# The tail of the attention stage put in the order in which its inputs arrive

## The chip, the cores and the metric

The kernel runs on one core of a Trainium2 chip. The metric is device time in microseconds (us), from three runs of the kernel. One more execution was taken with the profiler; all rows shown here come from that one.

## What is computed

The input is q, k, v for 4 batches, 8 heads, 576 positions and 64 values per head. Three stages follow each other, all in float32:

```
attn  softmax(scale * q k^T) v     heads 0-3: the last 32 positions; heads 4-7: every 4th of the last 128
x     2304 tokens x 512            (batch and position together, heads side by side)
moe   e = argmax(x @ w_gate);  gate = softmax(x @ w_gate)[e];  og = sigmoid(x @ w_output_gate)[e]
      y[token] = gate * og * (relu(x @ w1[e]) @ w2[e])          8 experts, 512 -> 1024 -> 512
moe2  out = softplus(y @ w_in) @ w_out                          512 -> 2048 -> 512
```

## The kernel before

**Attention.** The tokens are cut into 20 tiles (4 batches of five tiles, the fifth with 64 rows). A loop over `i` from 0 to 21 works on three tiles at once: scores and softmax of tile `i`, the transposed probabilities and the values of tile `i - 1` (`transpose_p`, `values`, `normalise`), and the transposed output of tile `i - 2` (`transpose_x`, `evict_x`). So the last tile, 19, is transposed in step 21, the last. In most steps two to four units of the next batch's q and k are transposed too (`transpose_qk`). The order of the instructions on TensorE (PE), ScalarE (ACT), VectorE (DVE) and the DMA queue of SyncE (SP) is the order in which the code is written; each of these engines works its list off in that order.

**PSUM.** Of the eight banks two belong to the scores (`ps_s`), one to the values (`ps_o`) and five to a ring (`ps_t`) that takes, one after the other, the transposed q and k (`pqk`), probabilities (`pp`) and outputs (`px`), the logits (`pl`, `plt`) and the ranks of the router (`prk`).

**Routing.** The tiles are routed in six groups; the last, group 5, is tiles 17 to 19. For a group, `logits` and `route` turn the transposed x into logits, the chosen expert, the token's place within it (`places`) and its weight (`pair`), in some 25 small DVE operations with one transpose (`plt`) and five small matmuls (`prk`) between them. They run as generators; `pump()` takes a few steps of them at fixed points of the loop. `scatter_idx` then writes the places and weights to DRAM (`idx_dram`) in one indirect DMA per tile from GpSimd (POOL). For group 5 that was put off to the end of the tail (`deferred`).

**The first expert.** After group 2 the expert with most tokens is taken as rank 0. Its first 424 token columns are put together on PE, without a trip through DRAM for the late tokens: `mm_gathered` (L968) adds rows of early tiles that were gathered from DRAM (`xg`, four tiles `t` of up to 128 rows), multiplied by a diagonal matrix of their weights (`diag`); `mm_late` (L1020) adds the rows of the late tiles 14 to 19, which are loaded (`load_late`, `xl`), scaled and split in a high and a low half (`split_late`: `h` on ACT, `l` on DVE) and multiplied by a selection matrix (`sel_late`, `sel`, on DVE). Tiles 14 and 19 have 64 rows each and share one operand. The four sums, one per 128 of the 512 values, stand in four accumulators `xacc` of one bank each: two in `ps_s`, one in `ps_o`, one in the ring.

**After that** `split_rank0` copies the accumulators out as `xh` (ACT) and `xl` (DVE), and the first expert's matmuls (`ph`, L900 to L902) begin. `order` sorts the experts by size on DVE, in small pieces during rank 0 (`tabi` is its result); from it SP reads which weights (`wr`) and which indices (`idx`) rank 1 needs. Weights come in pieces of 512 KB; `piece_hi` (ACT, `wh`) and `piece_lo` (DVE, `wl`) split them, and each `piece_lo` lets SP load one more.

What stands in step 20 and 21 and the tail is set by a table of events (`at(...)`), and the tail by a list `late` behind the loop (L1209 on), which is worked off while `pump()` moves group 5 along.

Of the kernel before, what the change touches and what calls it, by code (L numbers as in the profile page):

```python
# [14 lines left out]
I32 = mybir.dt.int32  # L15
# [27 lines left out]
def attn_moe_softplus_kernel(ctx: ExitStack, tc: tile.TileContext, q, k, v, w_gate, w_ogate, w1, w2, w_in, w_out, out, dbg=None):  # L43
# [257 lines left out]
    def transpose_qk(b, half, ti, y):  # L301

        ps = ps_t.tile([P, 512], F32, tag="tp", name=f"pqk{b}{half}{ti}{y}")

        def to(t, y):
            dst = qT[b % 2][64 * y : 64 * y + 64, half] if t == 0 else kT[b % 2][64 * y : 64 * y + 64, half, :, y]
            return dst[:, :, :S].rearrange("q x (p j) -> q x p j", j=9)

        if y < 2:
            r = raw[b, half, ti].rearrange("p y e -> p (y e)")
            for j in range(4):
                c = 2 * D * (5 * y + j)
# [166 lines left out]
    def transpose_x(b, w):  # L481
        d = tl[b, w]
        x2 = d["x"].rearrange("q a h d -> q (a h d)")
        ps = ps_t.tile([P, 512], F32, tag="tp", name=f"px{b}{w}")
        for c in range(4):
            nc.tensor.transpose(ps[:, P * c : P * c + P], x2[:, P * c : P * c + P], identf)
        d["xp"] = ps
# [59 lines left out]
    def route(g):  # L547
# [14 lines left out]
        d, eq, ex, sel, pm = t3("rd"), t3("req"), t3("rex"), t3("rsel"), t3("rpm")  # L562
        oh = t3("roh", BF16)
        cb = K["rt"].tile([P, NE], F32, tag="rcb", name=f"rcb{g}")
        posi = t2("rposi", I32)
        V.tensor_copy(lg[:, js], xT.pop(g)[:, :G4])
        yield 0
        R(mx, L, AX.X, ALU.max)
# [113 lines left out]

    def order():
        V = nc.vector
        pc = K["px"][0].tile([P, 512], F32, tag=K["px"][1], name="pcnt")[:, :NE]
        nc.tensor.matmul(pc, ones, cumb[:, len(GROUPS)], start=True, stop=True)

        def o3(nm):
            return K["rt"].tile([1, NE, NE], F32, tag=nm, name=nm, bufs=1)

        def o2(nm, n=NE):
            return K["rt"].tile([1, n], F32, tag=nm, name=nm, bufs=1)

        cnt, key, rank, g, r, lt, tmp, tab = o2("ocnt"), o2("okey"), o2("orank"), o3("og"), o3("or_"), o3("olt"), o3("otmp"), o2("otab", 40)
        ov = K["rt"].tile([1, NE, NT // OVW], F32, tag="oov", name="oov", bufs=1)
        thr = K["rt"].tile([1, NE, NT // OVW], F32, tag="thr", name="thr", bufs=1)
        for i in range(NE):
            nc.gpsimd.iota(thr[:, i], [[OVW, NT // OVW]], base=CAPS[i], channel_multiplier=0, allow_small_or_imprecise_dtypes=True)
        E0 = eidx[0:1]
        V.memset(tab, 0.0)  # L700
        V.scalar_tensor_tensor(key, pc[0:1], float(NE), rev[0:1], ALU.mult, ALU.add)
        V.scalar_tensor_tensor(key, first[0:1], float(2 * NE * NT), key, ALU.mult, ALU.add)
        V.tensor_copy(cnt, pc[0:1])
        yield
# [132 lines left out]
    def ntile(n):  # L837
        return (n + P - 1) // P
# [111 lines left out]
        nc.vector.tensor_scalar(d_[:rows], identf[:rows], idx[0].bitcast(F32)[:rows, t, 1:2], None, ALU.mult)  # L950

    def acc(c):
        pool, tag = ((ps_s, "s"), (ps_s, "s"), (ps_o, "o"), (ps_t, "tp"))[c]
        xacc[c] = pool.tile([P, 512], F32, tag=tag, name=f"xacc{c}")

    def acc0(c):
# [4 lines left out]
    def mm_gathered(cs):  # L961
        for c in cs:
            if c not in xacc:
                acc0(c)
        for t in range(ntile(CAPS[0])):
            rows = min(P, CAPS[0] - P * t)
            for c in cs:
                nc.tensor.matmul(  # L968
                    xacc[c][:, P * t : P * t + rows],
                    xg[0, t][:rows, P * c : P * c + P],  # L970
                    xacc["d", t][:rows, :rows],
                    start=False,
                    stop=False,
                    skip_group_check=True,
                )

    def rows_of(i):
        return P if i % NW < NW - 1 else S % P
# [230 lines left out]
    def w_lo(i, j):  # L1209
        lo_(0, j)  # L1210

    late = []
    for c in (2, 3):
        late += [(mm_late, 15, (c,), (0,)), (mm_gathered, NL, (c,))]
    late += [(mm_late, 15, (c,), (1,)) for c in (2, 3)] + [(mm_late, 15, (c,)) for c in (0, 1)] + [(mm_late, 16, (c,)) for c in range(NC)]
    late += [(fn, i) for fn in (sel_late, split_late) for i in range(17, n)] + [(w_lo, 17, j) for j in (0, 1)]
    late += [(mm_late, 17, (c,)) for c in range(NC)]

    late += [(mm_late, i, (c,)) for i, c in ((n - 2, 0), (n - 2, 1), (n - 1, 0), (n - 1, 1), (n - 2, 2), (n - 1, 2), (n - 2, 3), (n - 1, 3))]
    while late:  # L1220
        if bg:
            pump()
        fn, i, *a = late[0]
        g = next(g for g, (t0, t1) in enumerate(GROUPS) if t0 <= i < t1)
        if fn is mm_gathered or all(e[2] != g for e in bg):
            late.pop(0)
            fn(*a) if fn is mm_gathered else fn(i, *a)
    for fn in deferred:
        fn()
# [303 lines left out]
```

## Time and profile before

| | |
|---|---|
| median of the three runs | 806.53 us (804.1 to 810.0) |
| profiled execution | 803.44 us, of which the span from the first to the last instruction is 801.8 us |
| busy share of the span | PE 95%, DVE 68%, ACT 60%, POOL 15% |
| TensorE clock, mean of the span | 0.98 of full speed |

A row of the timeline gives the start, the length, the engine, the source line, the operation and its tiles; in brackets, how long the engine stood idle before it and what ended that. "x8" says that eight instructions in a row are shown as one; a matmul of float32 operands shows as two. "PEclk" is the granted clock: 1.00 is 2.4 GHz, 0.50 is 1.2 GHz.

### The profile page before, as it was taken

The page shows a single profiled execution, that of the slowest core. Times are in us where ns is not written, and L with a number is a line of the kernel's source. Part 1 is how long each engine was busy: PE and PEld are TensorE (multiplying, and loading weights), DVE is VectorE, ACT ScalarE, POOL GpSimd, SP SyncE. Part 2 cuts the span into 40 slices and gives each one's busy share as a digit, 9 for nine tenths or more (in the row PEclk, how much of TensorE's full clock was granted, in tenths as well). Part 3 has the DMA queues.
Part 4 walks back from the last instruction along what each step waited for, and adds up shares of the span by engine and source line. Part 5 has one row for each costly group of instructions (what it writes and reads, how often), then busy time and mean ns, then how long its engine had stood idle before and what let it go on. Part 6 is the DMA issues. An engine that isn't in the chain of part 4 may idle for free.

```text
span 801.8 us, 15124 instructions
## 1 busy us (share of the span) xinstructions
PE 764.0 (95%) x5542; PEld 690.7 (86%) x5543; DVE 548.5 (68%) x1098; ACT 479.3 (60%) x935; POOL 119.9 (15%) x154
## 2 busy tenths in 40 slices
PE   6998886999999999999999999999999999999994
PEld 4666665898999999999989999999998999999993
DVE  6967885763667977885698877766656656656561
ACT  4776642344556666666798878655556555655551
POOL 9814343121002011100000000110000001001001
PEclk8999997799999999999999999999999999999997
DMA  9996766255789999879524211310000001001001
GB/s 236 266 248 171 147 161 150 79 184 188 239 273 292 315 304 320 294 249 306 173 80 132 78 47 41 119 40 20 1 14 27 0 1 40 1 1 40 1 1 39
DMA packets 87008, 106.60 MB, mean 133 GB/s; under 512 B 30524, under 2 KB 61500, under 8 KB 86912
## 3 DMA queue, kind: packets, MB, share of 16 engines
q1 hardware_dynamic: 75616, 86.32, 36.9%
q0 software_dynamic: 5104, 13.40, 5.2%
q10 hardware_dynamic: 6192, 5.56, 2.0%
q8 instruction: 65, 1.06, 0.6%
q14 instruction: 31, 0.25, 0.1%
HBM read 85.03 MB, written 20.37 MB: 131 GB/s over the span
## 4 chain that ended last, share of the span: by engine, by line
PE 69%; issue 8%; DVE 5%; ACT 3%; DMA 2%; POOL 0%; ACTq 0%; SPq 0%; POOLq 0%; DVEq 0%
PE pg L900 7%; PE pg L901 7%; PE pg L902 7%; PE q L1442 7%; PE q L1441 7%; PE q L1443 7%; PE py L896 3%; PE py L897 3%; PE py L898 3%; PE ph L896 3%; PE ph L898 2%; PE ph L897 2%; PE ph L900 1%; PE ph L902 1%; PE ph L901 1%
## 5 line engine op out<-in xcount | busy, mean ns | idle before, releaser
L900 PE MATMUL pg<-xhm,wh 128*128 128x384 f32 x384 | 129.5, 337 | 0.5 <-ACT l L1408 0.4
L901 PE MATMUL pg<-xlm,wh 128*128 128x384 f32 x384 | 129.6, 338 | 0.0
L902 PE MATMUL pg<-xhm,wl 128*128 128x384 f32 x384 | 129.4, 337 | 0.0
L733 DVE TENSOR_TENSOR wl<-wr,wh 128x1024 fp32r<-128x1024 f32 (+1 forms) x86 | 98.2, 1144 | 30.7 <-ACT wh L788 30.6
L1406 ACT ACTIVATE u<-pg 128x384 f32<-128x384 f32 x96 | 47.2, 492 | 116.5 <-PE pg L902 116.4
L1442 PE MATMUL q<-wl,gh 128*128 128x512 f32 x288 | 113.2, 393 | 0.0
L1441 PE MATMUL q<-wh,gh 128*128 128x512 f32 x288 | 113.0, 393 | 0.0
L1443 PE MATMUL q<-wh,gl 128*128 128x512 f32 x288 | 112.6, 391 | 0.0
L788 ACT CAST wh<-wr 128x1024 fp32r<-128x1024 f32 x74 | 77.2, 1047 | 15.1 <-ACT y L923 5.2
L1450 POOL DMA_INDIRECT out_dram<-o,perm_sb x18 | 18.1, 1004 | 435.9 <-DVE o L260 303.2
L1412 DVE TENSOR_SCALAR w<-u 128x384 f32<-128x384 f32 x68 | 24.6, 362 | 84.7 <-ACT u L1407 84.2
L900 PEld LDWEIGHTS pg<-xhm,wh 128*128 128x128 f32 x384 | 72.1, 188 | 5.0 <-ACT l L1408 1.1
L901 PEld LDWEIGHTS pg<-xlm,wh 128*128 128x128 f32 x384 | 72.0, 188 | 3.7
L902 PEld LDWEIGHTS pg<-xhm,wl 128*128 128x128 f32 x384 | 72.1, 188 | 0.0
L1414 DVE SCALAR_TENSOR_TENSOR u<-w,u 128x384 f32<-128x384 f32 x96 | 53.7, 560 | 21.6 <-ACT w L1410 19.3
L1443 PEld LDWEIGHTS q<-wh,gl 128*128 128x128 f32 x288 | 54.1, 188 | 12.3
L1441 PEld LDWEIGHTS q<-wh,gh 128*128 128x128 f32 x288 | 54.1, 188 | 8.6
L1442 PEld LDWEIGHTS q<-wl,gh 128*128 128x128 f32 x288 | 54.0, 188 | 8.2
L896 PE MATMUL ph<-xh,wh 128*128 128x392 f32 (+5 forms) x192 | 58.6, 305 | 1.6 <-ACT y L923 0.9
L1416 DVE TENSOR_TENSOR l<-l,u 128x384 f32<-128x384 f32 x96 | 53.5, 557 | 7.7 <-ACT w L1420 0.5
L896 PE MATMUL py<-hh,wh 128*128 128x312 f32 (+8 forms) x192 | 58.4, 304 | 0.0
L897 PE MATMUL py<-hl,wh 128*128 128x312 f32 (+4 forms) x192 | 57.3, 299 | 0.1
(205 smaller groups left out, 1746.3 us busy)
## 6 DMA issues: line engine op xcount, KB each, us to landing
wr<-in_moe_w_dram SPq DMA_DIRECT2D x64, 512.0 KB, 6.1
praw<-in_moe_w_out_dram SPq DMA_DIRECT2D x12, 512.0 KB, 5.8
raw<-in_q_dram SPq DMA_DIRECT2D x8, 576.0 KB, 6.9
raw<-in_k_dram SPq DMA_DIRECT2D x8, 576.0 KB
x2r<-yT_dram SPq DMA_DIRECT2D x12, 384.0 KB, 4.2
vP<-in_v_dram SPq DMA_DIRECT2D x16, 272.0 KB, 9.0
praw<-in_moe_w_in_dram SPq DMA_DIRECT2D x8, 512.0 KB
wr<-in_moe_w_in_dram SPq DMA_DIRECT2D x8, 512.0 KB, 3.3
```

Source lines behind the costliest of these rows:

```text
L733: e.tensor_tensor(lo, src, hi.bitcast(F32), ALU.subtract)
L788: (eng or nc.scalar.copy)(d[1], d[0])
L896: nc.tensor.matmul(ps if wide else ps[:, :cut], wh, xh if wide else xh[:, :cut], start=wide, stop=False, skip_group_check=True)
L897: nc.tensor.matmul(ps[:, :cut], wh, xl[:, :cut], start=False, stop=False, skip_group_check=True)
L900: nc.tensor.matmul(ps, wh, xh, start=(first and i == 0), stop=False)
L901: nc.tensor.matmul(ps, wh, xl, start=False, stop=False)
L902: nc.tensor.matmul(ps, wl, xh, start=False, stop=(last and i == k - 1))
L1414: nc.vector.scalar_tensor_tensor(u, w_, 1.0, u, ALU.subtract, ALU.subtract)
L1416: nc.vector.tensor_tensor(l, l, u, ALU.subtract)
L1441: nc.tensor.matmul(acc[b, t], gh[:, ts_], wh, start=(f == 0), stop=False)
L1442: nc.tensor.matmul(acc[b, t], gh[:, ts_], wl, start=False, stop=False)
L1443: nc.tensor.matmul(acc[b, t], gl[:, ts_], wh, start=False, stop=(f == NF - 1))
```

## The change

**Events instead of a list.** The list `late` behind the loop is gone. All its work stands as events of step 21, in a new order, and `mm_gathered` does one gathered tile `t` per call for the accumulators that it is given. The scaling of tiles 14 to 16 (`sp`) is moved from step 20 behind the transposed x of tile 19. Group 5 is moved along by counted steps (`go`) between the matmuls.

**Banks.** The ring `ps_t` has four banks. The eighth bank is a pool of its own, `ps_x0`, for every transposed x (`px`), for two units of q and k at the start, and for the fourth accumulator.

**Counts and indices.** The first part of `order`, with its matmul `pcnt`, stands ahead of tile 19's matmuls and takes its bank from the ring. `scatter_idx` of group 5 follows the places at once, with an index tile of its own.

```
-    ps_t = psctx.enter_context(tc.tile_pool(name="ps_t", bufs=5, space=PSUM))
+    ps_x0 = psctx.enter_context(tc.tile_pool(name="ps_x0", bufs=1, space=PSUM))
+    ps_t = psctx.enter_context(tc.tile_pool(name="ps_t", bufs=4, space=PSUM))
...
+        own = b == 0 and (half, ti, y) in ((0, 0, 2), (1, 0, 2))
...
-        ps = ps_t.tile([P, 512], F32, tag="tp", name=f"px{b}{w}")
+        ps = ps_x0.tile([P, 512], F32, tag="x0", name=f"px{b}{w}")
...
-        posi = t2("rposi", I32)
+        posi = (const.tile([P, 4], I32, name="rposi_last")[:, :G4] if g == len(GROUPS) - 1 else t2("rposi", I32))
...
-        pc = K["px"][0].tile([P, 512], F32, tag=K["px"][1], name="pcnt")[:, :NE]
+        pc = ps_t.tile([P, 512], F32, tag="tp", name="pcnt")[:, :NE]
...
-        pool, tag = ((ps_s, "s"), (ps_s, "s"), (ps_o, "o"), (ps_t, "tp"))[c]
+        pool, tag = ((ps_s, "s"), (ps_s, "s"), (ps_o, "o"), (ps_x0, "x0"))[c]
...
-    at(20, 3, ("se", 14), ("se", 15), ("sp", 15, "hl"), ("sp", 14, "h"), ("se", 16), ("sp", 16, "h"), ("ll", 18), ("ll", 19))
-    at(21, 1, ("go", 5, 4), ("sp", 16, "l"), ("mg", 1), ("go", 5, 8), ("sp", 14, "l"))
+    at(20, 3, ("se", 14), ("se", 15), ("se", 16), ("ll", 18), ("ll", 19))
+    lo2, hi2 = (0, 1), (2, 3)
+    at(21, 1, ("sp", 15, "h"), ("mg", 0, lo2), ("sp", 15, "l"), ("mg", 1, lo2), ("go", 5, 3), ("ml", 15, (2,)), ("go", 5, 1))
+    at(21, 1, ("ml", 15, (3,)), ("sp", 14, "h"), ("go", 5, 8), ("ml", 15, lo2), ("mg", 2, lo2), ("go", 5, 1), ("sp", 16, "h"))
...
+    at(21, 1, ("sp", 14, "l"), ("q", 0), ("se", 19), ("sp", 18, "hl"), *(("ml", 18, (c,)) for c in range(4)))
+    at(21, 1, ("sp", 19, "hl"), ("or",), ("q", 1), *(("ml", 19, (c,)) for c in range(4)))
```

On ACT, where the x of tile 19 is transposed (`xT<-px`; the rows `h` scale tiles 15, 14 and 16). Before:

```order
L599 ACTIVATE rgs_2183<-rgs_2183 128x3
L999 ACTIVATE h_2290<-xl_15_2094,pair 128x512
L999 ACTIVATE h_2294<-xl_14_2011,pair 64x512
L999 ACTIVATE h_2299<-xl_16_2202,pair 128x512
L497 COPY xT_2147<-px_2310 128x512
L579 ACTIVATE rex_2341<-rd_2339 128x24
```

Now:

```order
L601 ACTIVATE rgs_2186<-rgs_2186 128x3
L499 COPY xT_2150<-px_2303 128x512
L1000 ACTIVATE h_2313<-xl_15_2097,pair 128x512
L1000 ACTIVATE h_2332<-xl_14_2014,pair 64x512
L581 ACTIVATE rex_2342<-rd_2340 128x24
```

The copy of tile 19 has moved ahead of the three rows that wait for loaded tiles.

On DVE, from the weights of group 5 (`pair<-rs`) to the first accumulator copied out (`xl<-xacc`). Before:

```order
L617 RECIPROCAL pair<-rs_2338 128x3
L1010 TENSOR_SCALAR sel_2400<-slots,rm_2335 128x424
L1010 TENSOR_SCALAR sel_2402<-slots,rm_2335 128x424
L1010 TENSOR_SCALAR sel_2286<-slots,rm_2335 64x424
L1001 SCALAR_TENSOR_TENSOR l_2406<-xl_17_2204,pair,h_2405 128x512
L1001 SCALAR_TENSOR_TENSOR l_2410<-xl_18_2302,pair,h_2409 128x512
L1001 SCALAR_TENSOR_TENSOR l_2295<-xl_19_2304,pair,h_2294 64x512
L733 TENSOR_TENSOR wl_0_2050<-wr_0_1763,wh_0_2049 128x1024
L733 TENSOR_TENSOR wl_1_2092<-wr_1_1765,wh_1_2091 128x1024
L629 CAST rposi_2346<-rm_2335 128x3
L733 TENSOR_TENSOR xl_2467<-xacc_2306,xh_2466 128x424
```

Now, up to the last row ahead of the expert counts, which wait for `pcnt`:

```order
L619 RECIPROCAL pair<-rs_2339 128x3
L1002 SCALAR_TENSOR_TENSOR l_2373<-xl_16_2205,pair,h_2372 128x512
L1011 TENSOR_SCALAR sel_2390<-slots,rm_2336 128x424
L631 CAST rposi_last<-rm_2336 128x3
L1002 SCALAR_TENSOR_TENSOR l_2397<-xl_17_2207,pair,h_2396 128x512
L1011 TENSOR_SCALAR sel_2412<-slots,rm_2336 128x424
L1002 SCALAR_TENSOR_TENSOR l_2333<-xl_14_2014,pair,h_2332 64x512
L736 TENSOR_TENSOR wl_0_2053<-wr_0_1766,wh_0_2052 128x1024
L1011 TENSOR_SCALAR sel_2289<-slots,rm_2336 64x424
L1002 SCALAR_TENSOR_TENSOR l_2428<-xl_18_2295,pair,h_2427 128x512
L1002 SCALAR_TENSOR_TENSOR l_2333<-xl_19_2297,pair,h_2332 64x512
L690 SCALAR_TENSOR_TENSOR okey<-pcnt,rev 1x8
```

Two more tiles' low halves (16 and 14) and a piece of weights stand between the weights of group 5 and the last low half; behind it come three rows of counts and the second piece (`wl_1`), then `xl`.

On PE, the end of the tail and the first expert's first matmuls, with the semaphores that a row waits for. Before:

```order
L686 MATMUL pcnt<-cumb,ones 128x8 [waits DVE_49]
L900 MATMUL ph_0_2543<-xh_2466,wh_0_2049 128x424 [waits DMAHW2_49,DMAHW1_49,DMAHW3_49,DMAHW0_49,DMAHW4_49,DMASW7_49,DMAHW5_49,DMASW6_49,DMAHW6_49,DMASW5_49,DMAHW7_49,DMASW0_49,DVE_49]
L901 MATMUL ph_0_2543<-xl_2467,wh_0_2049 128x424
L902 MATMUL ph_0_2543<-xh_2466,wl_0_2050 128x424
L900 MATMUL ph_0_2543<-xh_2466,wh_0_2049 128x424
L901 MATMUL ph_0_2543<-xl_2467,wh_0_2049 128x424
```

Now:

```order
L1021 MATMUL xacc_2329<-sel_2289,l_2333 128x424
L903 MATMUL ph_0_2551<-xh_2476,wh_0_2052 128x424 [waits DMAHW1_49,DMAHW2_49,DMAHW0_49,DMAHW3_49,DMASW7_49,DMAHW4_49,DMASW6_49,DMAHW5_49,DMASW5_49,DMAHW6_49,DMASW0_49,DMAHW7_49,DVE_49,Activation_49]
L904 MATMUL ph_0_2551<-xl_2477,wh_0_2052 128x424 [waits DVE_49]
L905 MATMUL ph_0_2551<-xh_2476,wl_0_2053 128x424
L903 MATMUL ph_0_2551<-xh_2476,wh_0_2052 128x424 [waits Activation_49]
L904 MATMUL ph_0_2551<-xl_2477,wh_0_2052 128x424 [waits DVE_49]
```

Before, one wait on DVE at the first matmul stood for everything behind it; now each quarter of `xh` and `xl` is waited for by the matmul that uses it.

## Rows read from the trace of the kernel before

**Rows 1.** The page: the span, and PE's busy time, share and instructions.

```profile
span 801.8 us, 15124 instructions
PE 764.0 (95%) x5542; PEld 690.7 (86%) x5543; DVE 548.5 (68%) x1098; ACT 479.3 (60%) x935; POOL 119.9 (15%) x154
```

**Rows 2.** Stretches: window, length, busy time per engine, PEclk, DMA share, GB/s.

```profile
131.50:135.00 3.50, 1.68 (x10) 1.06 (x9) 2.05 (x10) 1.23 (x2) 2.21 (x3) 0.99 0.92 302
135.00:148.60 13.60, 11.79 (x47) 9.78 (x48) 9.57 (x32) 3.78 (x8) 1.72 (x9) 0.50 0.38 64
148.60:155.40 6.80, 6.80 (x37) 6.46 (x36) 2.11 (x5) 1.44 (x3) 2.84 (x3) 1.00 0.46 155
```

**Rows 3.** The timeline of ACT in the tail: start, length, what, idle before.

```profile
133.77 1.33 ACT L999 ACTIVATE h<-xl,pair 128x512 fp32r<-128x512 f32 x2 [5.51 <-DMA xl<-x_dram]
136.08 0.72 ACT L999 ACTIVATE h<-xl,pair 128x512 fp32r<-128x512 f32 x1 [0.97 <-DMA xl<-x_dram]
136.71 0.56 ACT L497 COPY xT<-px 128x512 f32<-128x512 f32 x1
```

**Rows 4.** The timeline of PE in the tail.

```profile
131.84 0.66 PE L486 MATMUL px<-identf,x 128*128 128x128 f32 x4
...
137.32 1.92 PE L507 MATMUL pl<-xT,wg 128*32 128x128 f32 x8 [1.02 <-ACT xT L497]
...
142.92 2.06 PE L968 MATMUL xacc<-diag,xg 128*128 128x128 f32 x8
...
155.14 0.36 PE L1020 MATMUL xacc<-sel,l 128*128 128x424 f32 x1
...
156.74 0.47 PE L900 MATMUL ph<-xh,wh 128*128 128x424 f32 x1 [1.21 <-DVE xl L733]
```

**Rows 5.** The timeline of DVE in the tail and in rank 0.

```profile
134.52 0.75 DVE L1001 SCALAR_TENSOR_TENSOR l<-xl,pair,h 128x512 fp32r<-128x512 f32 x1 [1.42 <-ACT h L999]
...
140.47 0.20 DVE L566 COPY lg<-plt 128x48 f32<-128x48 f32 x1
...
142.00 0.73 DVE L1001 SCALAR_TENSOR_TENSOR l<-xl,pair,h 64x512 fp32r<-64x512 f32 x1
...
143.51 0.17 DVE L617 RECIPROCAL pair<-rs 128x3 f32<-128x3 f32 x1
143.60 1.21 DVE L1010 TENSOR_SCALAR sel<-slots,rm 128x424 fp32r<-128x424 f32 x3
144.85 2.19 DVE L1001 SCALAR_TENSOR_TENSOR l<-xl,pair,h 128x512 fp32r<-128x512 f32 x3
147.08 2.36 DVE L733 TENSOR_TENSOR wl<-wr,wh 128x1024 fp32r<-128x1024 f32 x2
...
154.20 1.71 DVE L733 TENSOR_TENSOR xl<-xacc,xh 128x424 fp32r<-128x424 f32 x3 [4.69 <-ACT xh L1033]
...
166.09 0.17 DVE L721 CAST tabi<-otab 1x40 int32<-1x40 f32 x1
```

**Rows 6.** The timeline of PE in two steps of the attention loop.

```profile
31.95 1.04 PE L315 MATMUL pqk<-identf,raw 128*128 128x128 f32 x8
33.27 0.66 PE L486 MATMUL px<-identf,x 128*128 128x128 f32 x4 [0.28 <-ACT kT L295]
...
38.00 0.60 PE L486 MATMUL px<-identf,x 128*128 128x128 f32 x4
```

**Rows 7.** The timeline of ACT in the same steps.

```profile
31.81 1.40 ACT L295 COPY kT<-pqk 64x512 f32<-64x512 f32 x2
36.96 0.59 ACT L497 COPY xT<-px 128x512 f32<-128x512 f32 x1
```

**Rows 8.** The queue of SP: the late tiles' last two loads, and rank 1's indices.

```profile
136.30 4.93 SPq L988 DMA_DIRECT2D xl<-x_dram  x2
167.30 0.39 SPq L740 DMA_DIRECT2D idx<-idx_dram  x1
```

**Rows 9.** The end of rank 0 on PE.

```profile
197.00 0.42 PE L896 MATMUL ph<-xh,wh 128*128 128x392 f32 x1 [0.86 <-ACT y L923]
```

More of the change, by code (lines that the diff above doesn't have):

```diff
@@ L301, in transpose_qk @@
     def transpose_qk(b, half, ti, y):
-        ps = ps_t.tile([P, 512], F32, tag="tp", name=f"pqk{b}{half}{ti}{y}")
+        own = b == 0 and (half, ti, y) in ((0, 0, 2), (1, 0, 2))
+        ps = (ps_x0 if own else ps_t).tile([P, 512], F32, tag="x0" if own else "tp", name=f"pqk{b}{half}{ti}{y}")
         def to(t, y):
@@ L684, in order @@
         V = nc.vector
-        pc = K["px"][0].tile([P, 512], F32, tag=K["px"][1], name="pcnt")[:, :NE]
+        pc = ps_t.tile([P, 512], F32, tag="tp", name="pcnt")[:, :NE]
         nc.tensor.matmul(pc, ones, cumb[:, len(GROUPS)], start=True, stop=True)
+        cnt, key = [const.tile([1, NE], F32, name=nm) for nm in ("ocnt", "okey")]
+        V.scalar_tensor_tensor(key, pc[0:1], float(NE), rev[0:1], ALU.mult, ALU.add)
+        V.scalar_tensor_tensor(key, first[0:1], float(2 * NE * NT), key, ALU.mult, ALU.add)
+        V.tensor_copy(cnt, pc[0:1])
+        yield
         def o3(nm):
@@ L692, in o2 @@
             return K["rt"].tile([1, n], F32, tag=nm, name=nm, bufs=1)
-        cnt, key, rank, g, r, lt, tmp, tab = o2("ocnt"), o2("okey"), o2("orank"), o3("og"), o3("or_"), o3("olt"), o3("otmp"), o2("otab", 40)
+        rank, g, r, lt, tmp, tab = o2("orank"), o3("og"), o3("or_"), o3("olt"), o3("otmp"), o2("otab", 40)
         ov = K["rt"].tile([1, NE, NT // OVW], F32, tag="oov", name="oov", bufs=1)
@@ L700, in order @@
         V.memset(tab, 0.0)
[L701 to L704, printed above, removed]
         V.tensor_tensor(g, bce(key, NE), bc(key, NE), ALU.is_gt)
@@ L959, in acc0, with mm_gathered @@
         nc.tensor.matmul(xacc[c][:, : CAPS[0]], ones, zero, start=True, stop=False, skip_group_check=True)
-    def mm_gathered(cs):
+    def mm_gathered(t, cs):
+        rows = min(P, CAPS[0] - P * t)
         for c in cs:
@@ L964, in mm_gathered @@
                 acc0(c)
[L965 to L975, printed above, removed]
+            nc.tensor.matmul(
+                xacc[c][:, P * t : P * t + rows],
+                xg[0, t][:rows, P * c : P * c + P],
+                xacc["d", t][:rows, :rows],
+                start=False,
+                stop=False,
+                skip_group_check=True,
+            )
     def rows_of(i):
@@ L1102, in attn_moe_softplus_kernel @@
     at(21, 0, ("az", 0), ("az", 1))
-    at(21, 1, ("mg", 0))
     for g, (t0, t1) in enumerate(GROUPS):
@@ L1114, in attn_moe_softplus_kernel @@
     at(20, 2, ("sc", 0), ("sc", 1), ("sc", 2), ("sc", 3))
-    at(20, 3, ("se", 14), ("se", 15), ("sp", 15, "hl"), ("sp", 14, "h"), ("se", 16), ("sp", 16, "h"), ("ll", 18), ("ll", 19))
-    at(21, 1, ("go", 5, 4), ("sp", 16, "l"), ("mg", 1), ("go", 5, 8), ("sp", 14, "l"))
+    at(20, 3, ("se", 14), ("se", 15), ("se", 16), ("ll", 18), ("ll", 19))
+    lo2, hi2 = (0, 1), (2, 3)
+    at(21, 1, ("sp", 15, "h"), ("mg", 0, lo2), ("sp", 15, "l"), ("mg", 1, lo2), ("go", 5, 3), ("ml", 15, (2,)), ("go", 5, 1))
+    at(21, 1, ("ml", 15, (3,)), ("sp", 14, "h"), ("go", 5, 8), ("ml", 15, lo2), ("mg", 2, lo2), ("go", 5, 1), ("sp", 16, "h"))
+    at(21, 1, *(("mg", t, hi2) for t in range(3)), ("go", 5, 9), ("sp", 16, "l"), ("se", 17), ("df",), ("sp", 17, "h"), ("mg", 3, (0, 1, 2, 3)))
+    at(21, 1, *(("ml", 16, (c,)) for c in range(4)), ("sp", 17, "l"), ("se", 18), *(("ml", 17, (c,)) for c in range(4)))
+    at(21, 1, ("sp", 14, "l"), ("q", 0), ("se", 19), ("sp", 18, "hl"), *(("ml", 18, (c,)) for c in range(4)))
+    at(21, 1, ("sp", 19, "hl"), ("or",), ("q", 1), *(("ml", 19, (c,)) for c in range(4)))
     ordering = order()
@@ L1133, in events @@
             elif what == "mg":
-                mm_gathered(a)
+                mm_gathered(*a)
+            elif what == "ml":
+                mm_late(*a)
             elif what == "ll":
@@ L1151, in events @@
                 split_late(*a)
+            elif what == "df":
+                deferred.pop()()
+            elif what == "or":
+                next(ordering)
     for i in range(n + 2):
@@ L1208, in attn_moe_softplus_kernel @@
             K["rt"] = K["rt2"]
[L1209 to L1229, printed above, removed]
     actx.close()
```

## The prediction

> **What bounds the kernel now.** I read the page first: PE is busy for 764.0 of 801.8 us [rows 1], so only work that is off PE's list, or a stretch where PE waits or runs slowly, can give time back. Then the windows over the tail, to see where that is: from 135.0 to 148.6 PE is busy for 11.79 of 13.60 us, but its granted clock is 0.50, the 1.2 GHz level; from 148.6 on it is 1.00 and PE is busy throughout [rows 2]. Then the timelines of ACT, PE and DVE there, to see what each is waiting for. The chain is: the transposes of tile 19 (`px`) end at 131.84 + 0.66 = 132.50 [rows 4]. ACT copies them out only at 136.71 [rows 3], since it stands behind three scalings `h`; their idle times, 5.51 and 0.97 us, end with loads of `xl` from DRAM. So the logits of tile 19 come at 137.32 and end at 139.24, DVE takes up the routing of group 5 at 140.47, and its weights are done at 143.68 [rows 4, 5]. PE does the gathered and late matmuls in that time, up to 155.14 + 0.36 = 155.50. The accumulators are copied out (`xl` from 154.20) and the first expert starts at 156.74, after 1.21 us in which PE waits for the last `xl` [rows 4, 5].
>
> **The wait removed.** The copy of tile 19 now stands ahead of the `h` rows: 136.71 - 132.50 = 4.2 us earlier. Nobody is pushed back by it: `h` of tile 15 waits for its load until 133.77 anyway, and the copy takes 0.56 [rows 3], to 133.1. The logits took 1.92 us at 0.50 [rows 4]; up to 135.0 the clock was 0.99 [rows 2], so half, 0.96: done at 134.05.
>
> **The routing of group 5.** On DVE the low half of tile 15 (134.52 to 135.27) stands ahead of it. From the end of the logits to `lg` it took 140.47 - 139.24 = 1.23 us, from there to the weights 143.68 - 140.47 = 3.21, of which some 0.7 was the low half of tile 14 that is no longer there (0.73) [rows 4, 5]. So `lg` at 136.5 and weights at 139.0. On PE, though, the ranks (`prk`) now stand behind six matmuls of tile 15 and two gathered pairs. At 1.00 a matmul of 424 columns takes 6.80 / 37 = 0.18 to 0.19 us [rows 2], at 0.50 twice that; a gathered block of eight records took 2.06 at 0.50 [rows 4]. From about 136.3 these are 6 x 0.37 + 1.0 = 3.2 us at 0.50, half at 1.00. The first delays the weights by about a microsecond, the second not at all: 139.0 to 140.2. I take 139.6, which is 4.1 earlier than before.
>
> **DVE behind the weights.** Up to the last low half there are five `l` at 2.19 / 3 = 0.73, three `sel` at 1.21 / 3 = 0.40, one `wl` at 1.18 and a small cast like `pair` (0.17) [rows 5]: 3.65 + 1.20 + 1.18 + 0.17 = 6.2, to 145.8. So the list is longer there than before (three `sel`, three `l`), and the 4.1 us shrink to 1.2: before, the last `l` ended at 147.04.
>
> **PE behind the ranks.** Two gathered blocks and some small pieces, 2.2 us at 1.00, then 24 late matmuls at 0.19, 4.6 us. The ranks end at 138 to 140, so PE is through with tile 18 at 145 to 147 if it has the upper level from about 140. Tile 18's low half comes from DVE 0.7 ahead of the last, at 145.1; seven matmuls behind it end at 146.4. `pcnt`, then eight matmuls of tile 19: 148.0. Before, that end was at 155.50, 7.5 us later, with the same matmuls.
>
> **The end.** After `pcnt` (146.5) DVE does three small counts, three times some 0.17, and the second `wl`, 1.18: 148.2. Here the change adds a wait: `wl` and all four `xl` are queued behind `pcnt`. Four `xl` at 1.71 / 3 = 0.57 end at 150.5, by when ACT has `xh`. The banks changed, too: the first expert's matmuls no longer wait for the last `xl` but quarter by quarter. Nine of its first twelve are done by then, so the twelfth starts at about 150.7. Before, it started at 156.74 + 11 x 0.19 = 158.8. That is 8.1 us. My chain has some ten hand-overs between engines that I put at nothing. The row of ACT's copy ends at 137.27 and PE starts at 137.32 [rows 3, 4], 0.05 later; where a matmul has to drain first it is more. I take 0.1 each, 1 us in all, so **7 us**.
>
> **The clock.** The upper level from 140 is the assumption. The trace of before has the lower one up to 148.6, in a tail with gathered blocks between; the new order has long runs of late matmuls from 136 on. A microsecond at 0.50 leaves half of its work undone. Up to 142 DVE's list covers that; if the lower level lasts to 148.6, PE owes (148.6 - 142) / 2 = 3.3 us, and the gain is 3.7. Ends: 3.7 and 8.1. I take 6.5, nearer to the upper.
>
> **The banks.** With five ring banks `px` at 33.27 waited 0.28 us for a copy of ACT [rows 6]. With four, the second of the two units ahead of it waits instead, and its four transposes (half of 1.04 us [rows 6], 0.5) move behind the wait. Such a step comes once per batch, three times: at most 1.6 us, and nothing where DVE is behind anyway; it could also give 0.3 back three times, since `px` has its own bank. I take a loss of 0.5. `px` in one bank must find the copy of the tile before done: it ended at 37.55 ahead of `px` at 38.00 [rows 6, 7], and that is the closest I found, so nothing.
>
> **Edits at nothing.** The index scatters go out some nine microseconds earlier; no one waits for them, since SP asks for rank 1's indices at 167.30, just after `tabi` (166.26) [rows 5, 8]. The counts' matmul is one small one either way. The load of tile 19 is issued at about 140.8 (second of two that end at 141.23 [rows 8]); with the 5 us that the load of tile 15 kept ACT waiting as a bound it is there by 146, so it may cost up to 0.9 by holding the last `l`; at 2 us nothing, and I put nothing.
>
> **Behind the tail** PE has the first expert's work without gaps until 0.86 us before 197.00 [rows 9]. Everything that feeds it hangs on DVE's list in rank 0 (`tabi`), which moves along, so the gain stays. The sum: 6.5 - 0.5 = 6.0, from 803.44 to **797.4** in an execution like the profiled one. The runs' median is 3.1 above that execution, so I forecast **800.4**.
>
> **The rivals.** Their times are those of the runs' median. *The clock stays low* through the tail, since PE still waits for DVE and loads in places. For it: a busy share of 11.79 / 13.60 did not raise it [rows 2]. Then 3.7 - 0.5 = 3.2 gained, or less: 803.3. Chance 0.27.
> *Rank 1 holds the gain back.* If its weights were late for a reason that does not move with the tail, PE would wait before 197 for what it gained: 806.5. Against it: SP's request at 167.30 follows `tabi` by 1.0 us [rows 5, 8]. Chance 0.08.
> *All goes well*: the upper level from 135, no bank is missed, and the wait of 0.86 us goes as well: 8.1 + 0.9 = 9, so 797.5. Chance 0.2.
> *The banks bind* (slower). The change takes all `px` out of the rotation and shortens the ring. Eleven steps have units of q and k, and a unit is copied in 1.40 us [rows 7]. If each such step lost one whole copy, 15 us would go, against 6.5: 815. It decides from 0.6 us a step on. Against it: with five banks PE waited 0.28 in such a step [rows 6]. Chance 0.04. (The Trainium skill, "Perfetto Trace Analysis", section "Matmuls", says that independent groups of matmuls should rotate through different PSUM banks, so that the copy of one overlaps the next group; by that rule this change goes the wrong way in the attention loop, and no row before shows a four-bank ring.)
> *My forecast* has 0.41.
>
> **How the numbers follow.** The forecast alone reaches from 797 to 803.5. The rivals add 797.5 down to 796 with the scatter of the runs, and 803.3 to 806.5; the slow case is left out. Range 795.5 to 806. A measurement here tells about 1% from no change, so faster means below 798.5: most of the 0.2 and a quarter of the forecast, 0.27. Slower by that is the slow rival alone, 0.04, and 0.01 for what I do not see. The rest, 0.68, is within 1%.
>
> **What would show it.** The copy of tile 19 on ACT at 132.5 with no load ahead of it; group 5's weights at 139 to 140.5; the clock in the windows 135 to 149; the last late matmul at 148 and the twelfth of the first expert at 151; PE's waits for ACT's copies before 118; `tabi` ahead of SP's request still. I am wrong if the routing is earlier and the first expert is not, or if PE shows new gaps between 20 and 118.

## The result and the profile after

The changed kernel takes **797.25 us** in the median (six runs, 796.48 to 798.06), the kernel before 806.39 (six runs, 804.1 to 810.0). The ratio is 0.9886, with a 95% interval of 0.9867 to 0.9906. In a second set of five runs (below) the change had 798.41, and a ratio of 0.9914 (0.9886 to 0.9941). The profiled execution is 796.84 us long, 6.6 less than that of before.

The page, its span and PE's busy time, in answer to [rows 1]:

```profile
span 795.0 us, 15124 instructions
PE 759.1 (95%) x5542; PEld 688.7 (87%) x5543; DVE 546.6 (69%) x1098; ACT 478.6 (60%) x935; POOL 119.4 (15%) x154
```

The windows of [rows 2], with the same columns:

```profile
131.50:135.00 3.50, 2.47 (x25) 1.48 (x16) 2.65 (x11) 1.56 (x3) 2.72 (x3) 1.00 0.94 294
135.00:148.60 13.60, 12.72 (x81) 11.53 (x80) 10.63 (x35) 4.26 (x10) 7.77 (x14) 1.00 0.59 143
148.60:155.40 6.80, 6.50 (x34) 5.98 (x34) 6.66 (x18) 5.50 (x9) 0.00 (x0) 1.00 0.79 157
```

Between 135.0 and 148.6 PE is busy for 12.72 us where it was for 11.79, but at the upper level throughout: 81 matmuls instead of 47.

ACT, in answer to [rows 3]; the copy follows the transposes (done at 132.74 + 0.66 = 133.40) at once:

```profile
133.44 0.59 ACT L499 COPY xT<-px 128x512 f32<-128x512 f32 x1 [2.92 <-PE px L488]
133.92 1.33 ACT L1000 ACTIVATE h<-xl,pair 128x512 fp32r<-128x512 f32 x2
...
144.43 0.72 ACT L1000 ACTIVATE h<-xl,pair 64x512 fp32r<-64x512 f32 x1 [2.87 <-DMA xl<-x_dram]
```

PE, in answer to [rows 4] and [rows 9]:

```profile
132.74 0.66 PE L488 MATMUL px<-identf,x 128*128 128x128 f32 x4 [0.35 <-DVE x L452]
134.07 1.06 PE L509 MATMUL pl<-xT,wg 128*32 128x128 f32 x8 [0.68 <-ACT xT L499]
...
136.26 0.71 PE L969 MATMUL xacc<-diag,xg 128*128 128x128 f32 x4 [0.48 <-DMA xg<-x_dram,idx]
...
145.48 0.46 PE L1021 MATMUL xacc<-sel,l 128*128 128x424 f32 x1 [0.40 <-DVE l L1002]
...
148.42 0.36 PE L1021 MATMUL xacc<-sel,l 128*128 128x424 f32 x1
148.61 0.35 PE L903 MATMUL ph<-xh,wh 128*128 128x424 f32 x1
149.27 0.46 PE L904 MATMUL ph<-xl,wh 128*128 128x424 f32 x1 [0.30 <-DVE xl L736]
...
151.30 0.36 PE L905 MATMUL ph<-xh,wl 128*128 128x424 f32 x1
...
189.45 0.42 PE L899 MATMUL ph<-xh,wh 128*128 128x392 f32 x1 [0.86 <-ACT y L926]
```

All waits left in the tail are under 0.7 us. The first expert begins before the last late matmul has ended (148.61, against 148.78), and its twelfth matmul starts at 151.30. Rank 1 begins at 189.45 instead of 197.00, behind the same 0.86 us.

DVE, in answer to [rows 5], and the queue of SP, in answer to [rows 8]:

```profile
140.01 0.18 DVE L619 RECIPROCAL pair<-rs 128x3 f32<-128x3 f32 x1
...
144.67 1.53 DVE L1002 SCALAR_TENSOR_TENSOR l<-xl,pair,h 128x512 fp32r<-128x512 f32 x2
147.15 0.15 DVE L690 SCALAR_TENSOR_TENSOR okey<-pcnt,rev 1x8 f32<-1x8 f32 x1 [0.95 <-PE pcnt L688]
...
148.63 2.10 DVE L736 TENSOR_TENSOR xl<-xacc,xh 128x424 fp32r<-128x424 f32 x4
...
157.69 0.17 DVE L724 CAST tabi<-otab 1x40 int32<-1x40 f32 x1
```

```profile
158.90 0.39 SPq L743 DMA_DIRECT2D idx<-idx_dram  x1
```

The weights of group 5 are done at 140.19, the last low half at 146.20, and `xl` waits for the counts. `tabi` still stands ahead of SP's request.

### The profile page after: what moved, and what is told of

It is laid out like the page before. It is cut to its first block, busy times and chain, and to the rows that moved or that the text cites. A ratio compares the mean times of both kernels' runs of the same rounds, so it can differ in the third digit from the quotient of the medians.

```text
span 795.0 us, 15124 instructions
## 1 busy us (share of the span) xinstructions
PE 759.1 (95%) x5542; PEld 688.7 (87%) x5543; DVE 546.6 (69%) x1098; ACT 478.6 (60%) x935; POOL 119.4 (15%) x154
## 4 chain that ended last, share of the span: by engine, by line
PE 68%; issue 8%; DVE 4%; DMA 4%; ACT 2%; another core or an unknown queue 1%; POOL 1%; SPq 0%; ACTq 0%; POOLq 0%; DVEq 0%
PE pg L903 7%; PE pg L904 7%; PE pg L905 7%; PE q L1432 7%; PE q L1433 7%; PE q L1434 7%; PE ph L899 3%; PE py L899 3%; PE ph L901 3%; PE py L900 3%; PE ph L900 3%; PE py L901 3%; DMA x_dram<-x 2%; PE ph L904 1%; PE ph L903 1%
```

## The experiments

Every run left a profile, and the tail can be cut in three pieces by rows like those above: **A** from the end of tile 19's transposes (`px`) to the weights of group 5 (`pair`), **B** from there to the end of the last late matmul, **C** from there to the start of the first expert's twelfth matmul. PEclk is the granted clock in B. The ratio is to the kernel before, run on the same chip, whose median there was 807.57 for banks alone, copy alone, wait back and old banks, 805.62 for the change again, copy, gathers, banks with zeros, gathers ahead and three moves, 806.79 for the four other kernels, so rows are compared by their ratios.

| kernel | A | B | PEclk | C | tail | this execution us | median us | ratio (95%) |
|---|---|---|---|---|---|---|---|---|
| before | 11.2 | 11.8 | 0.79 | 3.5 | 26.5 | 803.44 | 806.39 | 1 |
| the change | 6.8 | 8.6 | 1.00 | 2.5 | 17.9 | 796.84 | 797.25 | 0.9886 (0.9867 to 0.9906) |
| the change again | 6.0 | 8.6 | 1.00 | 2.5 | 17.2 | 798.16 | 798.41 | 0.9914 (0.9886 to 0.9941) |
| banks alone | 13.8 | 13.1 | 0.70 | 2.7 | 29.5 | 808.60 | 806.82 | 0.9985 (0.9971 to 0.9999) |
| copy alone | 12.8 | 11.9 | 0.79 | 3.5 | 28.2 | 807.16 | 807.03 | 0.9989 (0.9970 to 1.0008) |
| copy, gathers | 8.2 | 12.9 | 0.70 | 3.5 | 24.5 | 803.73 | 806.06 | 0.9985 (0.9965 to 1.0004) |
| copy, gathers, banks | 11.6 | 11.3 | 0.86 | 2.7 | 25.6 | 803.47 | 804.42 | 0.9975 (0.9958 to 0.9992) |
| the same with zeros | 10.2 | 13.5 | 0.70 | 2.7 | 26.5 | 802.09 | 802.08 | 0.9956 (0.9931 to 0.9981) |
| before with zeros | 13.6 | 8.7 | 1.00 | 3.5 | 25.8 | 802.61 | 806.32 | 1.0001 (0.9985 to 1.0016) |
| change, wait back | 11.8 | 8.4 | 1.00 | 2.5 | 22.8 | 805.30 | 804.33 | 0.9962 (0.9944 to 0.9980) |
| change, gathers ahead | 14.3 | 8.6 | 1.00 | 2.5 | 25.4 | 805.33 | 803.19 | 0.9959 (0.9934 to 0.9984) |
| change, old banks | 6.1 | 8.8 | 1.00 | 5.2 | 20.0 | 799.85 | 802.78 | 0.9950 (0.9929 to 0.9971) |
| the same with zeros | 6.7 | 12.7 | 0.90 | 3.8 | 23.2 | 802.58 | 800.40 | 0.9922 (0.9901 to 0.9944) |
| change, three moves | 6.7 | 8.2 | 1.00 | 2.2 | 17.0 | 793.92 | 797.25 | 0.9906 (0.9878 to 0.9935) |

A tail is that of one execution, a median that of 5 to 12 runs, so a row's tail and median need not move by the same amount. That execution is the shortest of its runs for before with zeros, old banks and three moves, and the longest for gathers ahead.

**Banks alone**, in the kernel before (with the two early units of q and k as in the change):

```
-    ps_t = psctx.enter_context(tc.tile_pool(name="ps_t", bufs=5, space=PSUM))
+    ps_x0 = psctx.enter_context(tc.tile_pool(name="ps_x0", bufs=1, space=PSUM))
+    ps_t = psctx.enter_context(tc.tile_pool(name="ps_t", bufs=4, space=PSUM))
...
-        ps = ps_t.tile([P, 512], F32, tag="tp", name=f"px{b}{w}")
+        ps = ps_x0.tile([P, 512], F32, tag="x0", name=f"px{b}{w}")
...
-        pool, tag = ((ps_s, "s"), (ps_s, "s"), (ps_o, "o"), (ps_t, "tp"))[c]
+        pool, tag = ((ps_s, "s"), (ps_s, "s"), (ps_o, "o"), (ps_x0, "x0"))[c]
```

> The kernel before with the banks of the change alone (four in the ring, the transposed x, two early units and the fourth accumulator in their own). My theory, banks nearly free: 0.5 us slower in the attention loop, up to 0.9 us given back where the first expert starts quarter by quarter, so 805.5 to 807.5 where the kernel before has 806.4; PE's waits for ACT's copies before 118 us grow by less than 2 us. Rival, the ring of four binds: 808 or more, and waits of pqk and px for ACT of 0.5 us and more in most steps. Rival, the start by quarters is a main part of the gain: 804 or less.

806.82 against 807.57: as expected. C is 0.8 shorter, since the first expert starts by quarters. In the loop the ring costs next to nothing: ahead of `pqk`, `px` and `pp` PE waits 1.8 us in all for ACT, where it was 1.4 (2.2 in the change).

**Copy alone.**

```
-    at(20, 3, ..., ("sp", 15, "hl"), ("sp", 14, "h"), ..., ("sp", 16, "h"), ...)
+    at(21, 1, ("sp", 15, "hl"), ("sp", 14, "h"), ("sp", 16, "h"), ("mg", 0))
```

> The kernel before with one move: the scalings of tiles 15, 14 and 16 stand behind the copy of tile 19's x; order, list and banks as before. My theory, the wait on ACT is one part and the order the other: the copy at 132.5, the routing 4 us earlier, and PE, which was idle for 3.6 us between 131.5 and 148.6, gives back 2 to 3.6 us of it: 802.5 to 804.5. Rival, the clock does it: without the wait the clock stays at 1.00 behind 135 us, and 6 to 8 us go: 798 to 800. Rival, the wait is covered by PE's other work: 806 to 807.

No difference: my theory missed. ACT copies at 132.76 now, and PE takes the logits 6.4 us later all the same:

```profile
132.07 0.66 PE L486 MATMUL px<-identf,x 128*128 128x128 f32 x4 [0.35 <-DVE x L450]
132.70 0.49 PE L968 MATMUL xacc<-diag,xg 128*128 128x128 f32 x2
135.18 0.49 PE L968 MATMUL xacc<-diag,xg 128*128 128x128 f32 x2 [2.00 <-DMA xg<-x_dram,idx]
136.71 0.55 PE L968 MATMUL xacc<-diag,xg 128*128 128x128 f32 x2 [1.03 <-DMA xg<-x_dram,idx]
138.60 0.65 PE L968 MATMUL xacc<-diag,xg 40*128 40x40 f32 x2 [1.34 <-DMA xg<-x_dram,idx]
139.18 1.91 PE L507 MATMUL pl<-xT,wg 128*32 128x128 f32 x8
```

Four gathered tiles stand ahead of the logits, and they wait for their gathers. Two waits stood beside each other, and the one on ACT hid the other.

**The wait put back** into the changed kernel:

```
-    at(20, 3, ("se", 14), ("se", 15), ("se", 16), ("ll", 18), ("ll", 19))
+    at(20, 3, ..., ("sp", 15, "hl"), ("sp", 14, "h"), ("se", 16), ("sp", 16, "h"), ...)
...
```

> The changed kernel with the three scalings put back ahead of the copy of tile 19's x, all else as changed. My theory: the weights of group 5 come about 4 us later, DVE's list of 6.2 us stands behind them, and 4 us of the gain go: 800.5 to 802 where the changed kernel has 797.3. Rival, the clock: if PE's longer wait brings the clock down to 0.50 in the tail, nearly all of the gain goes, 804 to 806. Rival, the order alone does it, and the wait is covered: 797 to 798.5.

804.33, the rival's number, but only half by its mechanism. ACT copies late again:

```profile
135.22 1.33 ACT L1000 ACTIVATE h<-xl,pair 128x512 fp32r<-128x512 f32 x2 [2.79 <-DVE pair L619]
137.94 0.72 ACT L1000 ACTIVATE h<-xl,pair 128x512 fp32r<-128x512 f32 x1 [1.39 <-DMA xl<-x_dram]
138.57 0.57 ACT L499 COPY xT<-px 128x512 f32<-128x512 f32 x1
```

A is 5.0 longer than in the change, B and C are as short as there. The clock fell (0.51 from 138.5 to 145.4 us), but before the weights, inside A. Of the 8.5 us between the two executions the tail has 4.9; 1.9 are there before `px` ends.

**Gathers ahead of the logits** in the changed kernel:

```
+    at(21, 1, *(("mg", t, (0,)) for t in range(4)))
-    ... ("mg", 0, lo2) ... ("mg", 1, lo2) ... ("mg", 2, lo2) ... ("mg", 3, (0, 1, 2, 3))
+    ... ("mg", 0, (1,)) ... ("mg", 1, (1,)) ... ("mg", 2, (1,)) ... ("mg", 3, (1, 2, 3))
```

> The changed kernel with one thing undone: the four gathered tiles of the first accumulator stand on PE ahead of the logits of tile 19, as they did before, instead of in pieces behind them. Theory, the landing of the gathers is a second wait of the same size behind the one on ACT, and it differs from execution to execution: the logits come 2 to 4 us later, the time is 800 to 803 and scatters by 3 us and more. Rival, the late matmuls of tile 15 fill the same time wherever the gathers stand: 797.5 to 799.

803.19, just above my range, with runs from 799.4 to 805.33. In the profiled execution, the longest of the ten, the wait is back, 4.91 us in three rows, and A is the longest of all, 14.3, with the clock at 0.50 from 134.5 to 144.8 us:

```profile
135.52 0.80 PE L969 MATMUL xacc<-diag,xg 128*128 128x128 f32 x2 [2.06 <-DMA xg<-x_dram,idx]
137.06 0.79 PE L969 MATMUL xacc<-diag,xg 128*128 128x128 f32 x2 [0.74 <-DMA xg<-x_dram,idx]
139.96 0.65 PE L969 MATMUL xacc<-diag,xg 40*128 40x40 f32 x2 [2.11 <-DMA xg<-x_dram,idx]
140.53 1.91 PE L509 MATMUL pl<-xT,wg 128*32 128x128 f32 x8
```

So both the copy and the gathers had to move; either one left in place costs half of the gain or more (0.9962 and 0.9959, where the change has 0.9886 and 0.9914).

**Copy and gathers moved, old list**, without and with the new banks:

```
-    at(21, 1, ..., ("mg", 0))
-    at(21, 1, ("go", 5, 4), ("sp", 16, "l"), ("mg", 1), ...)
+    at(21, 1, ("go", 5, 4), ("mg", 0), ("sp", 16, "l"), ("mg", 1), ...)
```

> The kernel before with the copy moved as in the first move, and the block of gathered rows of the first accumulator (four tiles) moved on PE from ahead of the logits of tile 19 to behind their transpose. Theory, two waits stood one behind the other: with the copy alone the logits waited for the gathers instead; with both out of the way the logits come at about 134.5, the weights of group 5 at 139.5 to 140.5, and PE gives back its 3 to 4 us of waiting: 802.5 to 805 where the kernel before has 807. Rival, the clock stays up once the logits are early: 799 to 801. Rival, the old list behind it takes up what is gained: 806 to 807.

> The same two moves and the banks of the change; what is still as before is the list of the tail, its order of late tiles on DVE and PE, the counts at the start of the first expert and the last index scatters. Theory: 1 us less than without the banks (the start by quarters), 801.5 to 804; the rest up to 798 is the interleaving of the late tiles with the routing and the clock. Rival, the interleaving is worth nothing: 797 to 799. Rival, banks pay only in the new order: as without them, 803 to 805.

806.06 and 804.42: both missed my theory and are the numbers of a rival. Without the banks A is 3 us shorter than before, but B is not:

```profile
142.44:155.30 12.86, 12.86 (x52) 0.70 0.31 87
```

(a window of PE alone: length, busy time, PEclk, DMA share, GB/s). PE works without a pause from the weights to the end, about three fifths of it at the lower level. With the banks A is long again in the profiled execution, for a third reason: DVE's low half of tile 15 stands ahead of `lt` and waits for ACT's scaling of it, and that for its load.

```profile
136.88 1.33 ACT L1001 ACTIVATE h<-xl,pair 128x512 fp32r<-128x512 f32 x2 [3.43 <-DMA xl<-x_dram]
137.63 0.75 DVE L1003 SCALAR_TENSOR_TENSOR l<-xl,pair,h 128x512 fp32r<-128x512 f32 x1 [3.61 <-ACT h L1001]
138.30 0.28 DVE L525 COPY lt<-pl 96x128 f32<-96x128 f32 x1
```

The changed kernel has this row order too (134.68, behind 0.32 us there): it is exposed to that load.

**Zeros in PE's waits.** `fill(k)` issues k bf16 matmuls of zeros into a bank that is free; in the kernel before at five places, 50 in all:

```
+    at(20, 1, ("fl", 8))
+    at(21, 0, ("fl", 4), ...)
+    at(21, 1, ("fl", 20), ("mg", 0), ("fl", 10))
+    at(21, 1, ("fl", 8), ("go", 5, 4), ...)
```

> The kernel before with 50 matmuls of zeros into banks that are free, put where PE waits between 124 and 140 us (for the transposed x, the gathers and the routing); nothing reads them, and nothing else is changed. They add about 5 us of PE work in waits of about 6 us. Theory, the lower clock of 13.7 to 17 us in the tail comes from those waits: the clock stays at 1.00 from 131 on, the 22 us of PE's work behind them run faster, and the kernel gets 3 to 6 us faster though it does more: 801 to 804. Rival, the clock is not brought down by the waits: no change or up to 2 us slower, 807 to 809, with 13 us at 0.50 in the tail again.

A miss in the time, 806.32 against 806.79, but for the most part not in the clock: it is at 0.50 for 3.4 us (from 138.6) instead of 13.6, and B is 8.7 instead of 11.8 to 13.1, with 1.00 all the way.

```profile
145.26:153.94 8.68, 8.68 (x48) 1.00 0.28 83
```

But in that execution the load for ACT's third scaling landed late, the copy started 6.6 us behind `px` (4.2 before), and the zeros themselves stand in PE's list, so A grew by 2.4. The clock shortens B; it can't help while A waits. That execution took 802.61 us, the shortest of the twelve; why the median stayed at 806.32 its profile cannot show.

The same in the kernel with copy, gathers and banks moved, 34 matmuls of zeros:

```
+    at(20, 1, ("fl", 8));  at(21, 0, ("fl", 4), ...);  at(21, 1, ..., ("fl", 6))
+    at(21, 1, ("fl", 8), ("go", 5, 4), ("fl", 8), ("mg", 0), ...)
```

> The kernel with the copy and the gathers moved and the new banks, but the old list, which had a median of 804.4; now with 34 matmuls of zeros in PE's waits between 126 and 139 us, some 3.5 us of work that nothing reads. Theory, the clock carries part of the gain: this kernel had 10.3 us at 0.50 from 137.3 on, with PE busy throughout from 140; if the zeros keep the clock at 1.00 there, up to 5 us go: 799.5 to 802. What is then left to the changed kernel (798) is its order of the late tiles. Rival, the clock follows the old list, or does not matter: 804 to 806.

802.08, just above the range, and the profiled execution does not show the step that I wanted: behind the zeros the last gathered tile still waited 2.95 us, and the clock fell there.

```profile
137.97 2.07 PE L970 MATMUL xacc<-diag,xg 40*128 40x40 f32 x10 [2.95 <-DMA xg<-x_dram,idx]
```

```profile
138.90:149.10 10.20, 10.20 (x40) 0.50 0.25 74
```

The times of its twelve runs go against their mean clocks with a correlation of -0.88, the strongest of the twelve sets of runs here (the others lie between -0.80 and 0.50): 804.62 and 807.17 at 0.982 and 0.983, and one run at 0.995 took 796.58, what the changed kernel takes. The mean clock counts the attention loop too, so this points to the clock and does not prove it.

**Old banks in the changed kernel:**

```
-    ps_x0 = ...;  ps_t = ...(name="ps_t", bufs=4, ...)
+    ps_t = ...(name="ps_t", bufs=5, ...)
...
-        ps = ps_x0.tile([P, 512], F32, tag="x0", name=f"px{b}{w}")
+        ps = ps_t.tile([P, 512], F32, tag="tp", name=f"px{b}{w}")
...
-        pool, tag = (..., (ps_x0, "x0"))[c]
+        pool, tag = (..., (ps_t, "tp"))[c]
```

> The changed kernel with the five-bank ring of the kernel before (transposed x and the fourth accumulator in the ring). My theory: the attention loop gets 0.5 to 0.9 us back, and the first expert again waits for the last low part, 0.7 to 1.2 us: 796.5 to 798.5, no difference. Rival, the own bank is what lets the new order run: 799.5 or more, with the first matmul of the first expert behind the last xl and waits for accumulator banks in the tail. Rival, the ring of four costs the 0.9 us by which the tail begins later in the changed kernel: 796.5 or less, with the transposes of tile 19 at 131.8 us again.

A miss: 802.78, not 797. In the new order DVE does the counts and a `wl` ahead of the four `xl`, and with the accumulator in the ring PE waits for the last of them, 2.03 us; then the clock falls, too. C is 2.6 longer than in the change in this execution, the shortest of the twelve; what the longer ones have besides is not shown.

```profile
150.98 0.46 PE L901 MATMUL ph<-xh,wh 128*128 128x424 f32 x1 [2.03 <-DVE xl L734]
```

```profile
152.10:155.50 3.40, 3.40 (x11) 0.51 0.92 178
```

With 15 matmuls of zeros in that wait:

```
+    fill(15, ps_t, "tp")
     actx.close()
...
     split_rank0()
```

> The changed kernel with the old five-bank ring, which had a median of 802.8, and 15 matmuls of zeros on PE between the last late matmul and the first expert, where it waits 2 us for the last low part; nothing reads them. Theory, that wait costs 1.7 us by itself and the rest of the 4.4 us through the clock behind it: 799.5 to 801 and less scatter, with no stretch at 0.50 behind 150 us. Rival, the ring itself costs the 4.4 us (accumulators or ranks that wait for a bank): 802.5 to 804.5.

800.40, as expected in time. But its profiled execution waits 1.91 us ahead of the last tile, whose load let ACT scale it only at 149.33, and has 0.50 behind it (151.1 to 154.5 us):

```profile
149.33 0.72 ACT L998 ACTIVATE h<-xl,pair 64x512 fp32r<-64x512 f32 x1 [5.02 <-DMA xl<-x_dram]
```

So whether the zeros helped through the clock stays open. The ring itself does not show as a cause: in A and B of these two profiles no matmul waits for a bank.

**Three small moves** in the changed kernel, and the change again beside it:

```
-    ("sp", 15, "l"), ("mg", 1, lo2), ("go", 5, 3), ("ml", 15, (2,)), ("go", 5, 1)
+    ("sp", 15, "l"), ("ml", 15, (2,)), ("mg", 1, lo2), ("go", 5, 4)
-    ("q", 0), ("se", 19), ("sp", 18, "hl")      ...      ("or",), ("q", 1)
+    ("se", 19), ("sp", 18, "hl"), ("q", 0)      ...      ("q", 1), ("or",)
```

> The changed kernel with three small moves for what its profile still shows as waits of PE in the tail: two matmuls of tile 15 ahead of the second gathered tile (0.48 us), the first piece of weights on DVE behind the low half of tile 18 (0.40 us), the second piece ahead of the counts that wait for their matmul (0.30 us). Theory: the three waits go and 0.4 to 1.1 us with them: 0.0005 to 0.0014 less than the changed kernel's ratio. Rival: the waits move to the next late input (the load of tile 19 or the last low part), no difference.

> The changed kernel itself, for its scatter and as the base of the run beside it. Theory, the scatter of the kernel before, 804 to 811, comes from its tail, where the waits for the gathers and the stretches at 0.50 differ, and the change takes it away: all runs within 796 to 799.5. Rival, the six runs seen so far were lucky: some of these lie at 800 to 804.

797.25 against 798.41, ratios 0.9906 and 0.9914, not told apart. In the profile PE's waits for the low half of tile 18 and for `xl` are gone, and that for the gathers has moved to the third tile (0.66 us). Two sets give eleven runs of the change, from 796.48 to 800.29; the 87 runs of the kernel before lie between 801.05 and 810.94. So the scatter is narrower, though one run passed my 799.5, and one of the six with three moves took 801.8.

## Why the prediction came out as it did

**The sum for the profiled execution held**: 6.6 us instead of 6.0. From `px` to the twelfth matmul 26.5 us became 17.9; 0.9 of that is taken back because `px` itself ends later (133.40, before 132.50), leaving 7.7 at the twelfth matmul; 7.55 is left at rank 1 and 6.8 at the end of the span. So the tail gave 2.1 more than the 6.5 that I took, and about as much went in places where the sum has only the 0.5 for the banks: that 6.6 is so near to 6.0 is in part luck.

- *The wait removed, the routing, DVE's list.* Predicted copy at 132.5, logits at 134.05, weights at 139.6, last low half at 145.8; found 133.44, 135.13, 140.19 and 146.20, from a `px` that ends 0.9 later. The sizes are right. The reading behind them was not complete: I took ACT's wait alone for the bound of the logits. The copy moved alone gives nothing, because the gathers stood next in line; the 4.2 us are real only since the change puts the gathered tiles behind the logits as well. The trace said so: PE itself stood idle for only 1.02 us for the copy that came 4.2 us late [rows 4], and two waits for the gathers stood ahead of it:

```profile
133.43 0.49 PE L968 MATMUL xacc<-diag,xg 128*128 128x128 f32 x2 [0.71 <-DMA xg<-x_dram,idx]
134.93 1.37 PE L968 MATMUL xacc<-diag,xg 128*128 128x128 f32 x4 [1.01 <-DMA xg<-x_dram,idx]
```

- *The clock.* Taken as 6.5 of 3.7 to 8.1; it stayed at 1.00 from 131.5 on. The rival with the lower clock is what the kernels with half of the change and the old list showed: B is 11.3 to 13.5 us at a PEclk of 0.70 to 0.86, and 8.2 to 8.8 at 1.00, in the old order (with zeros) as in the new. So of the 8.6 us in the tail 4.4 are A, 3.2 are B and 0.95 are C. Between the kernel with copy, gathers and banks (0.9975) and the change lie 5 to 7 us; how much of them is the order of the list and how much the clock was not separated.
- *The end.* Last late matmul 148.78 for 148.0, twelfth matmul 151.30 for 150.7. The 1 us for ten hand-overs was too much: behind a matmul, too, the next engine starts 0.03 to 0.04 us after the end that the profile gives it (`px` 133.40, copy 133.44; `pcnt` 147.12, counts 147.15). The quarters are worth 0.8 by banks alone, and 2.6 (C 5.2 instead of 2.5) once the counts stand ahead of `xl`. I had left that inside the 8.1 and given the banks only a loss.
- *The ring of four.* A loss of 0.5 was taken. The wait behind it is there: ahead of `pqk` PE waits for ACT's copies three times instead of once, while the 0.3 us ahead of `px` are gone (before, then now; us in all, times, longest):

```profile
PE pqk L323 <- ACT kT L295: 0.5, 1, 0.5
PE pqk L317 <- ACT kT L296: 1.7, 3, 0.7
```

In the time nothing shows. `px` of tile 19 ends at 131.2 to 135.3 us in the kernels with the new banks and at 132.5 to 134.2 in those with the old, zeros left out, and banks alone have 0.9985; a loss of 0.5 us could not be told from none there. The Trainium skill ("Perfetto Trace Analysis", section "Matmuls") has the rule that independent groups of matmuls should rotate through different PSUM banks, so that the copy of one overlaps the next group. The trace agrees in the waits, which grew by 1.2 us ahead of `pqk`; the kernel did not get slower by it, with 0.9985 for the banks alone.
- *Edits at nothing, rank 1.* In the tail no row waits for the index scatters; SP's request follows `tabi` by 1.0 us as before; the 0.86 us stay. The load of tile 19 cost no time in this execution (0.40 us went to the low half of tile 18), but 149.33 in another kernel shows that it can.

**The step that failed is the last one**: "The runs' median is 3.1 above that execution, so I forecast 800.4." The change's median is 0.4 above its profiled execution, and 0.25 in the second set. Of 87 runs of the kernel before 85 took longer than its profiled one, so that execution was an early one, and its tail shows in what: its gathered rows kept PE waiting for 1.7 us, where in two other profiles with that order (banks alone, copy alone) they did for 4.4, and its loads let ACT copy 4.2 us behind `px`, where it was 6.8 (banks alone) and 6.6 (before with zeros). Banks alone, whose `px` ends at 134.36:

```profile
138.22 0.49 PE L970 MATMUL xacc<-diag,xg 128*128 128x128 f32 x2 [3.53 <-DMA xg<-x_dram,idx]
139.57 1.38 PE L970 MATMUL xacc<-diag,xg 128*128 128x128 f32 x4 [0.86 <-DMA xg<-x_dram,idx]
141.13 0.57 ACT L499 COPY xT<-px 128x512 f32<-128x512 f32 x1
```

The new order has taken the logits out of both waits. So, as far as these profiles show, the change took away most of the offset that I added to it. They are of other kernels, though, that of banks alone 1.8 above its own median, and `px` itself ends 0.2 to 1.9 us later in banks alone and copy alone than in the kernel before, so a part of the offset can stand ahead of the tail. In the second set of runs the gain is 7.2 us (805.62 to 798.41), nearer to the 6.6 of the profiled executions than the 9.1 of the first. The rival in which all goes well (797.5) had the number, though not the reason: its 9 us were to come out of the profiled execution, which gave 6.6. That the whole scatter of the kernel before is in its tail was not shown, since only profiled executions can be cut in pieces.

## What to carry to other kernels

When a wait is removed, look for what stands next on the waiting engine's list: here three inputs (the copy, the gathers, a load ahead of `lt`) could each hold the same routing; the copy moved alone was worth nothing, and copy and gathers together next to nothing with the old list behind them. A difference between the median and the profiled execution can lie in waits that the change takes away: ask which waits on transfers make it, before adding it to a forecast. And in a PE-bound stretch behind a wait, see what clock is granted there: in six rows of the table B took 11.3 to 13.5 us at 0.70 to 0.86, where it takes 8.2 to 8.8 at 1.00.

## What the runs showed of the hardware

Once low, the clock stayed low under full load: 0.50 for 10.20 us in which PE was busy for 10.20 us (above), after a wait of 2.95 us. It also fell where PE had no such wait. In the change's second profile (PE alone, columns as above) PE's longest wait in the six microseconds before 129.9 was 0.84 us (most were under 0.7), and the tail behind it was as short as in the first, 17.2 us:

```profile
129.90:133.30 3.40, 3.40 (x40) 0.50 0.78 242
133.30:149.00 15.70, 14.53 (x93) 1.00 0.59 140
```

Where such a stretch falls differs between executions: the change has 0.50 in it at 109 to 113 us in one profile and at 130 to 133 in the other.
